# The opening of a fused attention and mixer kernel in another order: identity loaded by itself, first casts on other engines

## The chip, the core and the metric

The kernel runs on one core of a Trainium2 chip. Its time is the device time of one launch, in microseconds (us). The engines of the core are TensorE (PE), VectorE (DVE), ScalarE (ACT), GpSimd (POOL) and SyncE (SP); each works through its own instructions strictly in order and waits on semaphores for the others. SP, ACT and POOL also issue DMA transfers: SP and ACT each have a hardware queue, POOL a queue that is written by software. PE multiplies 16-bit matrices of 128 rows; a matmul takes about one column per clock, and the clock has two levels, 1.2 and 2.4 GHz.

## What is computed

The reference is attention with sliding windows, then a token mixer and a channel mixer, for 8 batches of 576 positions and 8 heads of 64:

```python
scores = scale * np.matmul(q, k.transpose(0, 1, 3, 2))          # per batch and head
mask_plain = (rel >= 0) & (rel < 32)                            # heads 0 to 3
mask_dil = (rel >= 0) & (rel < 128) & (rel % 4 == 0)            # heads 4 to 7
attn = softmax(np.where(masks, scores, -1e9)); attn_out = attn @ v
x = attn_out as (8, 576, 512)
h = np.maximum(xt @ w_tok1, 0.0) @ w_tok2                       # xt: x transposed, 576 -> 256 -> 576
u = x + h.transpose(0, 2, 1)
h2 = np.maximum(u @ w_ch1, 0.0) @ w_ch2                         # 512 -> 1536 -> 512
out = u + h2
```

Inputs and outputs are fp32; inside, operands are fp16 and sums fp32.

## The kernel before

**Staging.** One batch at a time goes through: load of q, k, v; casts to fp16 (`c_q`, `c_k`, `c_t` for the last 64 positions of q and k, `vv` and `vt` for the values); transposes by PE against an identity matrix (`tp_q`, `tp_k`, `tp_t`), copied to `qz` and `kt`; score products for pairs of heads (`sc`, `sm`) with a mask added by a product with `veil`; exponentials on ACT (`attp`, `attd`, `attt`); values times weights (`av`, value steps `va[0]` to `va[7]`, one for each head), divided by the row sum into `xn` on DVE; token mixer (`h1p`, then `h` by relu; `up`, then u); transposes of u (`uT`); and the channel mixer (`gp`, `gt` into hidden, `yp`, `yx`, `yw` out of it). The first matrices of the channel mixer (L941) and the last (L783) are the bulk of PE's work.

**What sets the order.** Nothing is scheduled by a tool: program order on each engine is the order of the source. For batch 0 there is nothing to overlap with, so its attention and token mixer, the *opening*, are written out one by one (L1009 to L1143). From there on `interleave(gen_main(b), steps)` merges the channel mixer of batch b with the attention of batches b+1 and b+2: each step carries a program time, such as `at(8.5, 0.7, dma_steps(b + 2))`, and is put where the running sum of PE's costs reaches it. These numbers only place instructions; at run time semaphores decide.

**The opening before.** POOL first issues the load of `const` (L1009: 672 columns: identity, permutation `perm`, mask band and tails, 168 KB), then clears buffers. SP issues the loads of q and v, ACT those of k. The hardware queues of SP and ACT rotate through 8 semaphores in the order of issue, so that a ninth transfer's issue waits until the transfer eight places earlier has landed; SP's loads of v (L211) stand behind such waits. PE runs nine products of the cleared buffer `idle` (`warm(9)`, L1004), then the transposes of head pair 0 (`tp(0)`), three more of the idle products, the scores of pair 0, and so on. The casts `c_q`, `c_k` of pair p are called by `cast_qk(0, "q", p, engine)`. `warm` does no useful work: it only keeps PE running.

**Names in what follows.** The heads go in pairs 0 to 3. In the list `ts` step 5p is `tp_q` of pair p, 5p+1 `tp_k` (L313), 5p+2 and 5p+3 the two halves of its scores (L427 mask, L429 product), 5p+4 its tails (`sm`). `first_tails` is `tp_t` and the copies of the tails (L415 to L422). `natural_w1` (L1073) reorders the first token matrix by products with `spread`. `emit_h1` is L637 and L639; `u_half(s, half)` makes one block of u (L1115 to L1123). `gate` (L1025) is a one-element copy on POOL into batch 1's load buffer, from `w2p`, so that SP's loads of batch 1 start behind it. `load_w3` are POOL's loads of the channel matrix. Behind the gate come POOL's casts of batch 1, in the order in which PE needs them.

Of the kernel before, what the change touches and what calls it, by code (L numbers as in the profile page):

```python
# [68 lines left out]
def kernel(  # L69
# [936 lines left out]
    ctx.enter_context(tc.manual_schedule())  # L1006


    nc.gpsimd.dma_start(out=const, in_=const_dram)  # L1009
    emit_fixed()  # L1010
    new_qk(0)
    load_qk(0, "q", 0, 2, nc.sync)
    load_qk(0, "k", 0, 2, nc.scalar)
    load_qk(0, "q", 2, 4, nc.sync)
    load_qk(0, "k", 2, 4, nc.scalar)
    load_tail(0, "q", nc.sync)
    load_tail(0, "k", nc.scalar)
    load_qk(0, "q", 4, 8, nc.sync)
    load_qk(0, "k", 4, 8, nc.scalar)
    spark = fixed("spark", [1, 1], FP32)  # L1020
    nc.scalar.activation(out=spark, in_=idle[0:1, 0:1], func=AF.Exp)
    load_v(0)

    def gate(t, src):
        nc.gpsimd.tensor_copy(out=t, in_=src)  # L1025
# [1 line left out]
    def load_w3(i):  # L1027
        c = slice(512 * i, 512 * i + 512)
        nc.gpsimd.dma_start(out=w3[i], in_=moe_w_ch1[:, c].rearrange("(x p) c -> p x c", p=128))

    cast_qk(0, "q", 0, nc.scalar)
    cast_qk(0, "k", 0, nc.vector)
    nc.vector.tensor_scalar(out=veil, in0=const[:, 256:CW], scalar1=1.0, scalar2=60000.0,
                            op0=ALU.subtract, op1=ALU.mult)
    cast_qk(0, "q", 1, nc.gpsimd)
    emit_fixed_late()
    cast_tails_qk(0, nc.gpsimd)
    nc.gpsimd.dma_start(out=w1p, in_=moe_w_tok1[0:512, :].rearrange("(m r) j -> m r j", r=4))
    for hp in range(2, 4):
        cast_qk(0, "q", hp, nc.gpsimd)  # L1040
    nc.gpsimd.dma_start(out=w1t[0][0:64], in_=moe_w_tok1[512:S, :])
    nc.gpsimd.tensor_copy(out=spread[:, 3:515:4], in_=ident)
    cast_qk(0, "k", 3, nc.gpsimd)
    for s in range(4):
        cast_vn(0, s, nc.gpsimd)
    nc.gpsimd.dma_start(out=w2a[:, :, 0:S], in_=moe_w_tok2.rearrange("(p j) t -> p j t", j=2))
    load_w3(0)
    cast_vd(0, 0, nc.gpsimd)
    cast_vd(0, 2, nc.gpsimd)
    load_w3(1)  # L1050
    cast_vx(0, nc.gpsimd)
    nc.gpsimd.dma_start(out=w1t[1][64:128], in_=moe_w_tok1[512:S, :])
    for jb in range(2):
        nc.gpsimd.tensor_copy(
            out=w2p[jb], in_=w2[jb][:, 0:512].rearrange("p (m r) -> p r m", r=4))

    warm(9)
# [3 lines left out]
    def tp(hp):
        ts[5 * hp]()
        ts[5 * hp + 1]()

    def sc(hp):
        for i in range(2, 5):
            ts[5 * hp + i]()

    def natural_w1(i):
        p = bank("main", 3, f"w1_p{i}")  # L1070
# [3 lines left out]
                                 lhsT=spread[:, 128 * s + 3 - r:128 * s + 131 - r], rhs=w1p[:, r],  # L1074
                                 start=(r == 0), stop=(r == 3))
        copy(nc.scalar, w1n[:, 2 * i:2 * i + 2].rearrange("p s j -> p (s j)"), p)

    tp(0)
    warm(3)
    ts[2]()  # L1080
    ts[3]()
    cast_qk(0, "k", 1, nc.vector)
    tp(1)
    first_tails()
    ts[7]()
    ts[8]()
    cast_qk(0, "k", 2, nc.vector)
    ts[10]()
    ts[4]()
    ts[9]()  # L1090
    ts[11]()
    tp(3)
    cast_tail_v(0, nc.vector)
    sc(2)
    natural_w1(0)
    va[0]()
    va[1]()
    sc(3)
    va[2]()
    va[3]()  # L1100
    natural_w1(1)
    for h in range(4, 8):
        va[h]()


    h1 = [sb.tile([128, DM], FP16, tag="h1", bufs=4, name=f"h1_0_{jb}") for jb in range(2)]
# [29 lines left out]
    for s in (1, 2):
        u_half(s, 1)
    for cb in (1, 2, 3):
        emit_uT(0, cb)
# [120 lines left out]
```

## Time and profile before

| what | value |
|---|---|
| runs (us) | 311.51, 277.65, 276.34; median 277.65 |
| profiled execution | 275.95 us, of which the span of its instructions is 274.1 us |
| PE busy in the span | 265.5 us (97%), 2694 matmuls |
| DVE, ACT, POOL busy | 168.4, 148.7, 159.9 us |
| chain that ended last | PE 89%, DMA 5%, DVE 2%, SP's queue 1%, ACT 1% |
| DMA | 54.98 MB, mean 201 GB/s |

The span is the time from the first instruction to the last; 1.85 us of the execution lie around it. An engine's busy time counts only instructions that do work. The chain is followed back from the last instruction, at each step to what released it, so that its shares say which engine's work or which transfer set the time there. Of the profile's 40 slices the first shows PE busy to six tenths, the second and the sixth to eight, the others up to the 39th to nine or more, and the last to four.

### The profile page before, as it was taken

What the parts mean: (1) busy time and instruction counts of PE and PEld (TensorE: products, weight loads), DVE (VectorE), ACT (ScalarE), POOL (GpSimd) and SP (SyncE); (2) the same over time, 40 slices, a digit from 0 to 9 for tenths busy, and PEclk for the clock granted to TensorE, in tenths of its full rate; (3) what the DMA queues carried; (4) which work ended last, traced back from release to release, by engine and by line L of the source; (5) the groups of instructions that cost most, each with busy time, mean ns of one, the idle gap of its engine ahead of it and who ended that gap; (6) DMA issues with size and microseconds to landing.
All of it is one profiled execution on the core that took longest, in us unless ns stands there. A gap on an engine that the chain in (4) does not pass through costs nothing.

```text
span 274.1 us, 6762 instructions
## 1 busy us (share of the span) xinstructions
PE 265.5 (97%) x2694; PEld 197.3 (72%) x2694; DVE 168.4 (61%) x340; ACT 148.7 (54%) x291; POOL 159.9 (58%) x216
## 2 busy tenths in 40 slices
PE   6899989999999999999999999999999999999994
PEld 2787676898676876687776876787776866786673
DVE  6667668676567656595557553875475464961363
ACT  2864675353674655467545666576646565236500
POOL 8871761289868659659974689749970870000000
PEclk9999999999999999999999999999999999999999
DMA  7999999995999799999999899979999040525015
GB/s 220 269 240 231 295 236 207 295 241 150 347 172 219 159 295 198 308 181 240 300 231 214 260 258 255 193 138 330 326 180 152 3 154 2 99 79 149 0 41 153
DMA packets 111471, 54.98 MB, mean 201 GB/s; under 512 B 82736, under 2 KB 107312, under 8 KB 111440
## 3 DMA queue, kind: packets, MB, share of 16 engines
q1 hardware_dynamic: 106784, 49.10, 77.0%
q0 software_dynamic: 2640, 3.94, 8.1%
q10 hardware_dynamic: 2016, 1.51, 1.8%
q8 instruction: 21, 0.34, 0.5%
q14 instruction: 10, 0.08, 0.1%
HBM read 37.59 MB, written 9.44 MB: 172 GB/s over the span
## 4 chain that ended last, share of the span: by engine, by line
PE 89%; DMA 5%; DVE 2%; SPq 1%; ACT 1%; issue 0%; ACTq 0%; POOL 0%
PE gp L941 30%; PE yx L783 13%; PE yw L783 9%; PE h1p L639 5%; PE up L651 4%; PE gt L932 4%; PE yp L969 4%; PE yp L752 4%; PE sc L524 3%; DMA lt<-in_k_dram 3%; DMA l_vx<-in_v_dram 2%; PE h1p L637 1%; PE av L621 1%; SPq L211 1%; PE av L616 1%; PE up L662 1%
## 5 line engine op out<-in xcount | busy, mean ns | idle before, releaser
L109 ACT ACTIVATE gt<-gp 128x512 f16<-128x512 f32 x89 | 53.3, 598 | 49.8 <-PE gp L941 49.5
L783 PEld LDWEIGHTS <-gt 128*128 128x128 f16 x600 | 57.0, 98 | 8.2
L941 PE MATMUL gp<-utd,w 128*128 128x512 f16 x144 | 54.7, 380 | 0.0
L941 PE MATMUL gp<-utm,w 128*128 128x512 f16 x144 | 54.6, 379 | 0.0
L941 PEld LDWEIGHTS <-w 128*128 128x128 f16 x384 | 39.0, 113 | 19.8 <-issue 0.5
L115 POOL TENSOR_TENSOR attp<-attp,const 128x1280 f16<-128x1280 f16 x12 | 31.6, 2637 | 22.1 <-ACT attp L549 22.1
L739 DVE TENSOR_TENSOR gt<-gt 128x768 f16<-128x768 f16 x56 | 32.5, 610 | 12.5 <-ACT gt L109 12.1
L115 DVE TENSOR_TENSOR xn<-av,rec 128x320 f16<-128x320 f32 x64 | 31.5, 492 | 2.2
L115 POOL TENSOR_TENSOR attd<-attd,const 128x1024 f16<-128x1024 f16 x12 | 25.5, 2127 | 5.9 <-issue 5.1
L941 PE MATMUL gp<-uT,w 128*128 128x512 f16 x96 | 25.8, 379 | 0.0
L796 DVE TENSOR_TENSOR o<-yx,u 128x512 f32<-128x512 f32 x22 | 15.2, 691 | 11.6 <-PE yx L783 11.4
L549 ACT ACTIVATE attp<-sc 128x480 f16<-128x480 f32 (+1 forms) x36 | 15.9, 538 | 8.8 <-PE sc L524 8.8
L783 PE MATMUL yx<-w,gt 128*128 128x256 f16 x168 | 20.6, 273 | 0.0
L783 PE MATMUL yx<-wsum_a,gt 128*128 128x256 f16 x168 | 20.6, 273 | 0.0
L657 DVE TENSOR_TENSOR u<-up,xn 128x512 f16<-128x512 f32 x26 | 17.8, 689 | 4.1 <-PE up L651 4.1
L628 DVE RECIPROCAL rec<-av 128x5 f32<-128x5 f32 x64 | 12.3, 192 | 12.7 <-PE av L625 12.6
L105 POOL CAST c_k<-l_k 128x512 f16<-128x512 f32 x29 | 17.6, 615 | 2.2 <-DMA l_k<-in_k_dram 1.1
L666 DVE TENSOR_TENSOR u16t<-up,xn 64x512 f16<-64x512 f32 x7 | 4.8, 690 | 20.8 <-PE up L662 20.8
L105 POOL CAST c_q<-l_q 128x512 f16<-128x512 f32 x26 | 16.3, 633 | 1.9 <-DMA l_q<-in_q_dram 1.2
L870 ACT COPY utd<-utm 128x512 f16<-128x512 f16 x12 | 12.7, 1125 | 8.8 <-DMA u<-utd 4.2
L109 ACT ACTIVATE h<-h1p 128x256 f16<-128x256 f32 x31 | 11.8, 384 | 9.5 <-PE h1p L639 9.1
L806 DVE TENSOR_TENSOR o<-yw,o 128x512 f32<-128x512 f32 x13 | 9.0, 692 | 10.2 <-PE yw L783 10.1
(159 smaller groups left out, 551.3 us busy)
## 6 DMA issues: line engine op xcount, KB each, us to landing
l_q<-in_q_dram SPq DMA_DIRECT2D x15, 512.0 KB, 6.4
l_k<-in_k_dram SPq DMA_DIRECT2D x14, 512.0 KB, 7.1
out_dram<-o SPq DMA_DIRECT2D x12, 512.0 KB, 4.6
l_vn<-in_v_dram SPq DMA_DIRECT2D x32, 128.0 KB, 6.8
l_vd<-in_v_dram SPq DMA_DIRECT2D x16, 256.0 KB, 5.1
w<-in_moe_w_ch_dram POOLq DMA_DIRECT2D x6, 512.0 KB, 7.8
out_dram<-o SPq DMA_DIRECT2D x17, 128.0 KB, 2.6
l_vt<-in_v_dram SPq DMA_DIRECT2D x8, 256.0 KB, 5.5
```

The costliest lines, as they stand in the source:

```text
L105: eng.tensor_copy(out=out, in_=in_)
L109: nc.scalar.activation(out=out, in_=in_, func=AF.Relu)
L115: eng.tensor_tensor(out=out, in0=x, in1=y, op=ALU.mult)
L549: nc.scalar.activation(out=out, in_=in_, func=AF.Exp, scale=0.125)
L628: nc.vector.reciprocal(out=rec[:, :, 0], in_=av[:, :, 64])
L639: nc.tensor.matmul(out=p, lhsT=w[:, s, j], rhs=x[:, s, c], start=False, stop=(s == 3))
L657: nc.vector.tensor_tensor(out=u16(b, s), in0=blocks4(p), in1=blocks4(xn[b][:, s]), op=ALU.add)
L739: nc.vector.tensor_tensor(out=out, in0=x, in1=y, op=op)
L783: nc.tensor.matmul(out=p, lhsT=gta[:, k0 + mb, r:r + 128], rhs=weights[:, mb, c], start=(first and not mb and (not a or len(parts) > 2)), ...
L796: nc.vector.tensor_tensor(out=o[i][:, :, 256 * j:256 * j + 256].rearrange("p s (x c) -> p s x c", x=2), in0=grid(p), in1=u, op=ALU.add)
L870: nc.scalar.copy(out=natural(uTd[:, cb - 2]), in_=uTm[i][:, cb].rearrange("p r m -> p m r"))
L941: nc.tensor.matmul(out=p, lhsT=w3_block(cb, mb), rhs=uT[(b, cb)][0], start=(i == 0), stop=(i == 3))
```

## The change

The opening is written in another order, and the numbers of the later batches are others. The identity (columns 0 to 127 of `const`, 32 KB) is loaded by itself on ACT's queue, the other 544 columns on POOL's. The cast `c_q` of pair 0 goes from ACT to DVE, `c_k` of pair 0 from DVE to POOL. The blocks of u, the steps of the scores and the loads of `w3` stand in other places. For the later batches the diff shows the numbers.

```diff
-    nc.gpsimd.dma_start(out=const, in_=const_dram)
-    emit_fixed()
...
-    cast_qk(0, "q", 0, nc.scalar)
-    cast_qk(0, "k", 0, nc.vector)
...
-    cast_qk(0, "q", 1, nc.gpsimd)
-    emit_fixed_late()
-    cast_tails_qk(0, nc.gpsimd)
...
-    tp(0)
-    warm(3)
-    ts[2]()
-    ts[3]()
-    cast_qk(0, "k", 1, nc.vector)
-    tp(1)
-    first_tails()
...
+    clear_gaps(attp[0])
+    nc.gpsimd.memset(idle, 0.0)
+    load_qk(0, "q", 0, 2, nc.sync)
+    nc.vector.memset(qza[0:64, :, 1], 0.0)
+    nc.gpsimd.dma_start(out=const[:, 128:], in_=const_dram[:, 128:])
...
+    load_qk(0, "k", 2, 4, nc.scalar)
+    load_tail(0, "q", nc.sync)
+    nc.scalar.activation(out=spark, in_=idle[0:1, 0:1], func=AF.Exp)
+    nc.scalar.dma_start(out=const[:, 0:128], in_=const_dram[:, 0:128])
+    nc.gpsimd.memset(vv[0][:, :, :, 64:65], 1.0)
+    load_tail(0, "k", nc.scalar)
+    load_qk(0, "k", 4, 8, nc.scalar)
...
+    cast_qk(0, "k", 0, nc.gpsimd)
+    nc.vector.memset(attt, 1.0)
+    nc.gpsimd.memset(spread, 0.0)
+    clear_gaps(attp[1])
+    cast_tails_qk(0, nc.gpsimd)
+    cast_qk(0, "q", 0, nc.vector)
+    cast_qk(0, "q", 1, nc.gpsimd)
...
+    ts[0]()
...
+    warm(3)
+    ts[1]()
+    cast_qk(0, "k", 1, nc.vector)
+    ts[2]()
+    ts[5]()
+    ts[6]()
+    first_tails()
+    ts[7]()
+    cast_qk(0, "k", 2, nc.vector)
+    ts[8]()
+    ts[9]()
+    ts[10]()
+    ts[3]()
...
-    for s in (0, 2):
-        u_half(s, 0)
...
-    for s in (4, 1, 3):
-        u_half(s, 0)
-    for s in (4, 3, 0):
-        u_half(s, 1)
+    u_half(2, 0)
+    u_half(3, 0)
+    u_half(4, 0)
+    emit_h1(0, 0, 1, h1[0])
+    emit_h1(0, 1, 1, h1[1])
+    u_half(1, 0)
+    u_half(0, 0)
+    u_half(3, 1)
+    u_half(4, 1)
+    u_half(0, 1)
...
-                steps += at(14.6 + late / 6, 0.0, [lambda b=b: u_natural(b)])
+                steps += at(12.75 + late / 6, 1.6, [lambda b=b: u_natural(b)])
...
-                    b + 1, 5.4 + late / 6, 8.2 + late / 6, 10.6 + late / 6, 22.4 + late, 0.9, 4.1, 1.0)
+                    b + 1, 5.0 + late / 6, 8.75 + late / 6, 10.6 + late / 6, 23.2 + late, 0.9, 4.95, 0.4)
...
-                steps += at(2.0, 0.6, cast_steps(b + 2)) + score_steps(b + 2, 21.4 if b % 2 else 18.0, 8.4 if b % 2 else 6.4)
+                steps += at(2.15, 0.95, cast_steps(b + 2)) + score_steps(b + 2, 20.2 if b % 2 else 18.4, 6.1 if b % 2 else 6.4)
...
-                steps += at(8.5, 0.7, dma_steps(b + 2)) + at(12.0, 0.4, places[:4])
-                steps += at(19.6 if b % 2 else 17.2, 0.0, places[4:])
+                steps += at(7.7, 0.8, dma_steps(b + 2)) + at(15.0, 0.0, places[:4])
+                steps += at(19.2 if b % 2 else 17.2, 2.85, places[4:])
...
-                steps += at(17.6, 0.9, load_steps(b + 3))
+                steps += at(19.1, 2.0, load_steps(b + 3))
```

The queue of ACT at the start, before, in the order in which ACT takes it (`lt` holds the last 64 positions of q and k; `spark` is one exponential that makes ACT load its table):

```order
L194 DMA l_k<-in_k_dram 128x2x256 x2
L200 DMA lt<-in_k_dram 64x8x64
L194 DMA l_k<-in_k_dram 128x4x256
L1021 ACT_TABLE_LOAD
L1021 ACTIVATE spark<-idle 1x1
L103 CAST c_q<-l_q 128x512
L103 COPY qz<-tp_q 64x512 x2
```

The same place of ACT's queue with the change:

```order
L194 DMA l_k<-in_k_dram 128x2x256 x2
L1068 ACT_TABLE_LOAD
L1068 ACTIVATE spark<-idle 1x1
L1069 DMA const<-consts 128x128
L200 DMA lt<-in_k_dram 64x8x64
L194 DMA l_k<-in_k_dram 128x4x256
L103 COPY qz<-tp_q 64x512 x2
```

The load of the table, `spark` and the new load of the identity now stand ahead of the load of `lt`, and the cast of `c_q` is gone from this engine.

On POOL, from the first cast of the opening to the loads behind it, before (the cast `c_q` at the top is pair 1's; `c_t` is the cast of `lt`):

```order
L105 CAST c_q<-l_q 128x512
L177 MEMSET vv 128x40
L178 MEMSET vt 64x4
L179 MEMSET w1t 128x256
L177 MEMSET vv 128x40
L178 MEMSET vt 64x4
L179 MEMSET w1t 128x256
L180 MEMSET w 128x2x64
L105 CAST c_t<-lt 128x512
L1038 DMA w1p<-in_moe_w_tok_dram 128x1024
L105 CAST c_q<-l_q 128x512 x2
```

The same part of POOL's program with the change:

```order
L105 CAST c_k<-l_k 128x512
L1086 MEMSET spread 128x515
L1021 MEMSET attp 128x8x128
L105 CAST c_t<-lt 128x512
L105 CAST c_q<-l_q 128x512
L1091 MEMSET vv 128x40
L1093 MEMSET w 128x2x64
L1095 MEMSET w1t 128x256
L1096 MEMSET vt 64x4
L1097 DMA w1p<-in_moe_w_tok_dram 128x1024
L105 CAST c_q<-l_q 128x512
```

The cast `c_q` of pair 1 has gone behind `c_t`, which reads both tails; `c_k` of pair 0 has come to the top; four of the small memsets now stand between `c_q` of pair 1 and the load of `w1p`.

## Rows read from the trace of the kernel before

**Rows 1.** Stretches: from:to, length, then busy us (instructions) of each engine, clock, DMA.

```profile
10.00:12.00 2.00, 1.50 (x23) 1.29 (x22) 1.73 (x6) 1.91 (x5) 1.73 (x4) 1.00 1.31 249
...
28.00:45.00 17.00, 16.24 (x199) 11.67 (x198) 11.38 (x26) 11.37 (x23) 10.13 (x20) 1.00 1.12 250
45.00:260.00 215.00, 215.00 (x2136) 159.79 (x2133) 130.58 (x258) 121.95 (x236) 131.56 (x155) 1.00 0.87 198
260.00:274.10 14.10, 10.43 (x96) 8.18 (x93) 7.23 (x15) 0.00 (x0) 0.00 (x0) 1.00 0.32 94
```

**Rows 2.** Chain that ended last, its longest piece: start, length, what.

```profile
1.80 7.03 DMA lt<-in_k_dram
```

**Rows 3.** Timeline of PE: start, length, line, operation, count, [idle before <-releaser].

```profile
2.54 4.02 PE L1004 MATMUL idle_p<-idle 128*128 128x512 f16 x9 [2.54 <-POOL idle L164]
6.60 0.59 PE L313 MATMUL tp_q<-const,c_q 128*128 128x128 f16 x4
...
7.40 1.05 PE L1004 MATMUL idle_p<-idle 128*128 128x512 f16 x3
...
8.40 0.24 PE L429 MATMUL sc<-qz,kt 128*128 128x160 f16 x1
...
9.17 0.39 PE L313 MATMUL tp_q<-const,c_q 128*128 128x128 f16 x4
...
10.56 0.24 PE L429 MATMUL sc<-qz,kt 128*128 128x160 f16 x1 [0.49 <-DVE kt L318]
...
13.58 0.25 PE L429 MATMUL sc<-qz,kt 128*128 128x128 f16 x1 [0.26 <-DVE kt L318]
...
19.49 0.19 PE L625 MATMUL av<-vt,attt 128*128 128x65 f16 x1 [0.53 <-POOL vt L105]
...
31.57 0.39 PE L313 MATMUL tp_k<-const,c_k 128*128 128x128 f16 x4
```

**Rows 4.** DMA transfers by issue: what, queue, count, KB, us from issue to landing.

```profile
l_k<-in_k_dram ACTq DMA_DIRECT2D x1, 256.0 KB, 4.7
const<-consts POOLq DMA_DIRECT2D x1, 168.0 KB, 5.3
...
lt<-in_k_dram ACTq DMA_DIRECT2D x1, 128.0 KB, 7.0
...
w1t<-in_moe_w_tok_dram POOLq DMA_DIRECT2D x1, 32.0 KB, 5.2
```

**Rows 5.** Timeline of ACT and DVE in the first 16 us, columns as in PE's.

```profile
0.73 1.03 ACTq L194 DMA_DIRECT2D l_k<-in_k_dram  x2
...
3.44 1.28 ACT L1021 ACT_TABLE_LOAD   x1 [3.44 <-issue]
...
5.97 0.35 DVE L105 CAST c_k<-l_k 128x512 f16<-128x512 f32 x1
...
7.65 0.69 DVE L318 COPY kt<-tp_k 128x512 f16<-128x512 f16 x1 [0.74 <-PE tp_k L313]
...
15.41 0.45 DVE L105 CAST vv<-l_vt 128x512 f16<-128x512 f32 x1 [1.29 <-DMA l_vt<-in_v_dram]
```

**Rows 6.** Timeline of POOL, the same columns.

```profile
8.88 0.61 POOL L105 CAST c_t<-lt 128x512 f16<-128x512 f32 x1 [0.80 <-DMA lt<-in_k_dram]
...
14.13 0.72 POOL L1046 DMA_DIRECT2D w<-in_moe_w_tok_dram  x1
...
21.30 0.18 POOL L1025 CAST lt<-w2p 1x1 f32<-1x1 f16 x1
...
30.09 1.17 POOL L105 CAST c_k<-l_k 128x512 f16<-128x512 f32 x2 [0.17 <-DVE gt L111]
```

**Rows 7.** Timeline of PE and ACT in an odd batch.

```profile
146.70 2.75 PE L752 MATMUL yp<-w,gt 128*128 128x512 f16 x12
...
147.39 1.08 ACT L103 COPY kt<-kr 128x512 f16<-128x512 f16 x1
...
149.38 0.65 PE L524 MATMUL sc<-qt,kt 64*128 64x160 f16 x14
```

More of the change, by code (lines that the diff above doesn't have):

```diff
@@ L1006 @@
     ctx.enter_context(tc.manual_schedule())
-    nc.gpsimd.dma_start(out=const, in_=const_dram)
-    emit_fixed()
     new_qk(0)
[L1012 to L1019, printed above, removed]
     spark = fixed("spark", [1, 1], FP32)
-    nc.scalar.activation(out=spark, in_=idle[0:1, 0:1], func=AF.Exp)
-    load_v(0)
+    v_loads = load_v_steps(0)
     def gate(t, src):
@@ L1029, in load_w3, with clear_gaps, make_veil @@
         nc.gpsimd.dma_start(out=w3[i], in_=moe_w_ch1[:, c].rearrange("(x p) c -> p x c", p=128))
-    cast_qk(0, "q", 0, nc.scalar)
-    cast_qk(0, "k", 0, nc.vector)
-    nc.vector.tensor_scalar(out=veil, in0=const[:, 256:CW], scalar1=1.0, scalar2=60000.0,
-                            op0=ALU.subtract, op1=ALU.mult)
-    cast_qk(0, "q", 1, nc.gpsimd)
-    emit_fixed_late()
-    cast_tails_qk(0, nc.gpsimd)
[L1038 to L1057, printed above, removed]
+    def clear_gaps(a):
+        nc.gpsimd.memset(a.rearrange("p h (b c) -> p h b c", c=PST)[:, :, :, 128:PST], 0.0)
+    def make_veil():
+        nc.vector.tensor_scalar(out=veil, in0=const[:, 256:CW], scalar1=1.0, scalar2=60000.0,
+                                op0=ALU.subtract, op1=ALU.mult)
     ts = [st[2] for st in score_steps(0, 0.0, 1.0)]
     va = [st[2] for st in value_steps(0, 0.0, 1.0)]
[L1061 to L1067, printed above, removed]
+    h1 = [sb.tile([128, DM], FP16, tag="h1", bufs=4, name=f"h1_0_{jb}") for jb in range(2)]
     def natural_w1(i):
@@ L1076, in natural_w1 @@
         copy(nc.scalar, w1n[:, 2 * i:2 * i + 2].rearrange("p s j -> p (s j)"), p)
-    tp(0)
-    warm(3)
-    ts[2]()
-    ts[3]()
-    cast_qk(0, "k", 1, nc.vector)
-    tp(1)
-    first_tails()
[L1085 to L1106, printed above, removed]
     def u_half(s, half):
@@ L1123, in u_half @@
             nc.vector.tensor_tensor(out=t[rows], in0=blocks4(p[rows]), in1=blocks4(xn[0][rows, s, c]), op=ALU.add)
-    for jb in range(2):
-        emit_h1(0, jb, 0, h1[jb])
-    for s in (0, 2):
-        u_half(s, 0)
-    for jb in range(2):
-        emit_h1(0, jb, 1, h1[jb])
-    for s in (4, 1, 3):
-        u_half(s, 0)
-    for s in (4, 3, 0):
-        u_half(s, 1)
-    emit_uT(0, 0)
[L1136 to L1139, printed above, removed]
+    clear_gaps(attp[0])
@@ new lines @@
+    nc.gpsimd.memset(idle, 0.0)
+    load_qk(0, "q", 0, 2, nc.sync)
+    nc.vector.memset(qza[0:64, :, 1], 0.0)
+    nc.gpsimd.dma_start(out=const[:, 128:], in_=const_dram[:, 128:])
+    nc.vector.memset(qza[64:128, :, 0], 0.0)
+    load_qk(0, "k", 0, 2, nc.scalar)
+    load_qk(0, "q", 2, 4, nc.sync)
+    nc.gpsimd.memset(vt[1][64:128], 0.0)
+    load_qk(0, "k", 2, 4, nc.scalar)
+    load_tail(0, "q", nc.sync)
+    nc.scalar.activation(out=spark, in_=idle[0:1, 0:1], func=AF.Exp)
+    nc.scalar.dma_start(out=const[:, 0:128], in_=const_dram[:, 0:128])
@@ new lines @@
+    nc.gpsimd.memset(vv[0][:, :, :, 64:65], 1.0)
+    load_tail(0, "k", nc.scalar)
+    load_qk(0, "k", 4, 8, nc.scalar)
+    load_qk(0, "q", 4, 8, nc.sync)
+    v_loads[0]()
+    nc.gpsimd.memset(vt[0][64:128], 0.0)
+    v_loads[1]()
+    v_loads[2]()
+    v_loads[3]()
+    v_loads[4]()
+    v_loads[6]()
+    v_loads[5]()
+    nc.gpsimd.memset(vt[0][0:64, :, 64:65], 1.0)
+    nc.gpsimd.memset(w1t[0], 0.0)
+    cast_qk(0, "k", 0, nc.gpsimd)
+    nc.vector.memset(attt, 1.0)
+    nc.gpsimd.memset(spread, 0.0)
@@ new lines @@
+    clear_gaps(attp[1])
+    cast_tails_qk(0, nc.gpsimd)
+    cast_qk(0, "q", 0, nc.vector)
+    cast_qk(0, "q", 1, nc.gpsimd)
+    nc.gpsimd.memset(vv[1][:, :, :, 64:65], 1.0)
+    v_loads[7]()
+    nc.gpsimd.memset(w2a[:, :, S:640], 0.0)
+    make_veil()
+    nc.gpsimd.memset(w1t[1], 0.0)
+    nc.gpsimd.memset(vt[1][0:64, :, 64:65], 1.0)
+    nc.gpsimd.dma_start(out=w1p, in_=moe_w_tok1[0:512, :].rearrange("(m r) j -> m r j", r=4))
+    cast_qk(0, "q", 2, nc.gpsimd)
+    nc.gpsimd.tensor_copy(out=spread[:, 3:515:4], in_=ident)
@@ new lines @@
+    cast_qk(0, "q", 3, nc.gpsimd)
+    cast_qk(0, "k", 3, nc.gpsimd)
+    cast_vn(0, 0, nc.gpsimd)
+    nc.gpsimd.dma_start(out=w1t[0][0:64], in_=moe_w_tok1[512:S, :])
+    cast_vn(0, 2, nc.gpsimd)
+    cast_vn(0, 3, nc.gpsimd)
+    cast_vn(0, 1, nc.gpsimd)
+    nc.gpsimd.dma_start(out=w2a[:, :, 0:S], in_=moe_w_tok2.rearrange("(p j) t -> p j t", j=2))
+    load_w3(0)
+    cast_vd(0, 0, nc.gpsimd)
+    cast_vd(0, 2, nc.gpsimd)
+    warm(9)
+    cast_vx(0, nc.gpsimd)
+    load_w3(1)
+    nc.gpsimd.tensor_copy(out=w2p[1], in_=w2[1][:, 0:512].rearrange("p (m r) -> p r m", r=4))
@@ new lines @@
+    ts[0]()
+    nc.gpsimd.tensor_copy(out=w2p[0], in_=w2[0][:, 0:512].rearrange("p (m r) -> p r m", r=4))
+    nc.gpsimd.dma_start(out=w1t[1][64:128], in_=moe_w_tok1[512:S, :])
+    warm(3)
[11 more added lines that the diff above has]
+    ts[3]()
+    ts[11]()
+    ts[15]()
+    ts[16]()
+    ts[4]()
+    cast_tail_v(0, nc.vector)
+    ts[12]()
+    ts[13]()
@@ new lines @@
+    ts[14]()
+    natural_w1(0)
+    va[0]()
+    va[1]()
+    ts[17]()
+    ts[18]()
+    ts[19]()
+    va[2]()
+    va[3]()
+    natural_w1(1)
+    va[4]()
+    va[5]()
+    va[6]()
+    va[7]()
+    emit_h1(0, 0, 0, h1[0])
+    emit_h1(0, 1, 0, h1[1])
+    u_half(2, 0)
[8 more added lines that the diff above has]
+    u_half(0, 1)
+    emit_uT(0, 0)
+    u_half(1, 1)
+    u_half(2, 1)
@@ L1142 @@
+    emit_uT(0, 1)
+    emit_uT(0, 3)
+    emit_uT(0, 2)
     new_qk(1)
```

## The prediction

> **What bounds the kernel now.** I read the stretches first. From 45 to 260 us PE is busy 215.00 of 215.00 us at the full clock [rows 1]: a reader should see that nothing there can be won by another order of the same matmuls, and the change keeps them all. The end, 14.1 us with PE busy 10.43, has no step that moves. What is left is the opening and its handover to batch 1 (28 to 45: PE 16.24 of 17.00). The chain of waits names what sets the opening: the transfer of k's tails, from its issue at 1.80 to its landing at 8.83 [rows 2]. PE's timeline then gives the size of each wait: it idles 0.49 us ahead of the product at 10.56, 0.26 ahead of 13.58 and 0.53 ahead of 19.49 [rows 3]. So the question is where the start of the channel mixer, near 27 us, goes; behind it every microsecond counts once.
>
> The sum is made against the profiled execution, 275.95 us (span 274.1, and 1.85 around it). The median of the runs shown is 277.65, the faster of the other two 276.34. Two per cent, about what a measurement of this kernel can tell from no change, is 5.5 us.
>
> **Identity.** Before, it landed with all of `const`, at 1.22 + 5.3 = 6.5, and PE's first transposes began at 6.60 [rows 3, 4]. Now ACT issues two loads of k (until 1.76), loads its table (1.28) and then issues the identity's 32 KB, at about 3.2 [rows 5]. Below, it can't come ahead of the load of k in front of it on that queue, which was issued near 1.25 and took 4.7: 5.95 [rows 4, 5]. Above, the nearest transfer of the same size took 5.2, which gives 8.4 [rows 4]. I go by the queue itself: the tails' 128 KB, in the same rows of 256 bytes, landed 2.88 behind that load of k; a quarter of the bytes, a quarter of the time, 0.7: 6.7. The cast of `c_q` on DVE is hidden: it takes the slot of `c_k` there, 5.97 to 6.32 [rows 5]. First transposes at 6.75: **+0.15**.
>
> The Trainium skill, "DMA: Bandwidth & Descriptors", section "Anatomy of one DMA — SWDGE (gpsimd) path", gives a fit of about 2.0 us plus bytes over 436 GB/s. By it the identity would land near 5.3 and the transposes begin with the cast, at 6.4, 0.2 earlier than before. The trace doesn't bear it out in this stretch: 32 KB took 5.2 and 168 KB 5.3 on POOL's own queue.
>
> **First scores.** `warm(3)`, 1.05 us, now stands between `tp_q` and `tp_k` of pair 0. Before, it lay behind both and hid the copy to `kt` [rows 3]; now nothing hides that copy. The two transposes took 0.80 together (6.60 to 7.40), so `tp_k` moves from 7.0 to 6.75 + 0.4 + 1.0 = 8.15. The copy began 0.65 behind it [rows 5]; at the full clock four transposes take 0.39 and not 0.59 [rows 3], so say 0.45 now: 8.6 to 9.3, first product at 9.3 and not 8.40, **+0.9**. `c_k` of pair 0 goes to POOL, 0.61 like `c_t` [rows 6]; its data are there by 4.5 and it is needed at 8.15, so it costs nothing unless POOL's memsets run three microseconds late. The mask's columns now go second on POOL; even 1 us late they land near 7.6, ahead of 9.3.
>
> **Pair 1.** On POOL `c_q` of pair 1 now stands behind `c_t`, which needs k's tails. On ACT these now stand behind the table and the identity. Below: 8.0; `const` now starts about 1 us later on POOL, and its 168 KB at the profile's mean of 201 GB/s are 0.84 us of the transfers that shared the time with the early loads. Above: issued near 3.7, 7.0 on the way as before [rows 4], 10.7. I take the identity's 0.7 on top of 8.83: 9.55, since the queue was busy from the first load on. Two casts of 0.61 [rows 6] and `tp_q` of pair 1 starts at 10.85, not 9.17: **+1.65**. PE has only half of pair 0's scores to do until then (0.4, from 9.3 to 9.7): a **new wait of about 1.1 us**. Transposes, copy and product follow as before, 10.56 + 1.65 = 12.2 [rows 3].
>
> **Pair 2.** Until 13.58 before there were 3.02 us, 0.26 of them idle [rows 3]. The second half of pair 0's scores, 0.4, is new in there, and `tp_q` of pair 2 stands behind pair 1's tails, so that DVE gets its copies later. Between 0 (all of it under DVE's copies) and 0.4 (none) I take 0.35: pair 2 **+2.0**.
>
> **Given back.** The values of the dilated heads waited 0.53 for `vt`, whose data came late; when PE comes 2 us later, they are there. The cast of `l_vt`, done at 15.86 [rows 5], released the first values; what PE lost there lies between 0 and the 0.26 of its neighbour; I take 0.2. The new order of u's blocks puts another block behind the relu; from -0.3 to +0.3, I take -0.2. The start of the channel mixer: 2.0 - 0.53 - 0.2 - 0.2 = **+1.05**.
>
> **Handover to batch 1.** POOL's load of the second token matrix goes from 14.13 to about 16.0: tails 0.7, the cast of pair 1 that is now behind them 0.6, four small memsets that were ahead of them about 0.6. `w2p` and the gate at 21.30 [rows 6] follow, to about 23.2, or 23.7 with the load that now stands right ahead of the gate. SP's loads of batch 1 are all queued behind the gate. Their first cast of `c_k` was done at 30.7 (30.09 + 0.61), its transposes began at 31.57 [rows 3, 6]: 0.87 to spare, 1.9 with PE's own delay. A shift of 1.9 to 2.4 costs 0 to 0.5: **+0.2**.
>
> **Later batches.** An odd batch's first group of dilated scores stands four matmuls earlier, 2.75 / 12 × 4 = 0.9. ACT's copy to `kt` ended at 148.47, the scores began at 149.38 [rows 7]: just enough. If it isn't, a wait of at most the copy's 1.08 in each of two batches. Loads that stand later behind SP's output stores have most of a batch to spare. I take 0 (bounds 0 and +2.2; a gain is excluded by PE's 215.00).
>
> **Sum:** 1.05 + 0.2 = +1.25, so 275.95 + 1.25 = **277.2**.
>
> **Rivals.**
>
> *The opening gets shorter.* If the early loads gain what `const` took from them, the tails land near their lower end, 8.0. Pair 1 starts at 9.7, held by its first scores and the two casts, not by 1.1 us of waiting; pair 2 comes at most 0.5 later, and the waits that vanish (0.53 + 0.2) and u's 0.2 make it -0.4 to -0.9. Time 275.3. For it: PE's order now has work for each copy of DVE. Against it: the tails were the last to land before, and two more things stand ahead of them. Chance 0.24.
>
> *The other side: batch 1's loads.* If identity and tails come at their upper ends (8.4 and 10.7), POOL's program shifts by 1.2 more, the gate goes to about 24.7, 3.4 later than before; pair 1's start goes to 12.0, and the mixer to +2.2. The transposes of batch 1's k then lack 3.4 - 0.87 - 2.2 = 0.3, and each later cast of POOL, which follow each other closely, keeps the lag. 2.2 + 0.3 to 1.3 gives 278.5 to 279.5. It decides at 0.87 us: a gate that is later than PE's mixer by more than that stops PE. For it: the 5.2 us of 32 KB. Against it: the transfers of one queue share its time, so a late issue costs less than it is late. Chance 0.16.
>
> *The clock falls back.* The products at the start ran at the lower level, 4.02 us for nine [rows 3]. PE now idles about 0.9 and 1.1 us between 8.5 and 10.85 with 0.4 of work between. From 10 to 12, PE was busy 1.50 of 2.00 us and the clock stayed at 1.00 [rows 1], which speaks against it; but that stretch was denser. At the lower level five microseconds of matmuls cost 2.5 more; less what waits hide, 279.3. Chance 0.06. The Trainium skill, "TensorE: Matmul & The Clock Gate", section "Why this matters for your kernels", warns that idle gaps between bursts of matmuls take PE back to its slow clock, which speaks against an order with two such waits; before, no row shows such a fall.
>
> *It doesn't do what it says:* the identity lands no earlier than the whole `const` did, because it is queued behind k. That is already my forecast.
>
> **How the numbers follow.** The forecast of 277.2 has 0.50 (its own range 276.2 to 278.5), the rivals 0.24, 0.16 and 0.06, other mishaps of the later batches 0.04. The range runs from the shorter opening's lower part, 274.9, to the late loads' upper end, 279.5. No case reaches 5.5 us but several together: faster 0.02, same 0.94, slower 0.04.
>
> **What would show it.** Right: first transposes at 6.6 to 6.9 and `tp_k` behind the three idle products; PE's wait ahead of `tp_q` of pair 1, released by POOL's `c_q`; no wait for `vt` near 20; the gate near 23; PE full from 45 to 260. Wrong: tails that land before 8.9 (then the first rival), `tp_k` of batch 1 waiting for POOL by over half a microsecond (the second), a clock under 1.00 near 11 (the third), or idle PE in the dilated scores of the odd batches.

## The result and the profile after

The changed kernel took 280.44 us (median of 6 runs, 279.79 to 281.71) beside 277.24 of the kernel before: a ratio of 1.0131, interval 1.0094 to 1.0168, or 3.6 us more. It is slower, as forecast, and within 2%, but above the range that was given (up to 279.5) and three times the forecast step (+1.25). Ratios leave disturbed runs out: for one experiment below too few were left for a ratio, and the profiles of 5, 6, 8 and 10 are of such runs (287 to 288 us), so that the lengths of those four profiles aren't compared with the others'.

The stretches of the changed kernel's profile (span 278.6), columns as in [rows 1]:

```profile
10.00:12.00 2.00, 1.23 (x12) 0.78 (x11) 1.13 (x2) 0.33 (x1) 1.66 (x5) 1.00 1.23 283
28.00:45.00 17.00, 15.63 (x180) 10.84 (x178) 10.60 (x22) 11.21 (x23) 10.50 (x20) 1.00 1.11 255
45.00:260.00 215.00, 213.19 (x2132) 158.35 (x2130) 134.97 (x261) 120.53 (x233) 134.71 (x156) 1.00 0.86 201
260.00:279.00 19.00, 14.89 (x135) 11.43 (x132) 8.92 (x18) 2.64 (x5) 0.00 (x0) 0.97 0.23 70
```

Two things changed: PE does less from 28 to 45 us (15.63 for 16.24), and it has lost 1.81 us in the middle, which was full before. The chain that ended last says where, among its longest pieces:

```profile
2.57 7.64 DMA lt<-in_k_dram
25.10 8.24 DMA l_k<-in_k_dram
...
125.28 2.82 DVE gt L739
```

k's tails are on it as before, 7.64 us and from a later issue; a load of batch 1 is new on it, and one sum of DVE. PE's timeline, against [rows 3]:

```profile
2.20 4.02 PE L1004 MATMUL idle_p<-idle 128*128 128x512 f16 x9 [2.20 <-POOL idle L1058]
7.77 0.59 PE L313 MATMUL tp_q<-const,c_q 128*128 128x128 f16 x4 [1.54 <-DMA const<-consts]
8.15 1.48 PE L1004 MATMUL idle_p<-idle 128*128 128x512 f16 x3
9.43 0.63 PE L313 MATMUL tp_k<-const,c_k 128*128 128x128 f16 x4
10.85 0.31 PE L429 MATMUL sc<-qz,kt 128*128 128x160 f16 x1 [0.65 <-DVE kt L318]
11.76 0.40 PE L313 MATMUL tp_q<-const,c_q 128*128 128x128 f16 x4
13.16 0.24 PE L429 MATMUL sc<-qz,kt 128*128 128x160 f16 x1 [0.49 <-DVE kt L318]
16.64 0.24 PE L429 MATMUL sc<-qz,kt 128*128 128x128 f16 x1 [0.26 <-DVE kt L318]
...
21.71 0.19 PE L625 MATMUL av<-vt,attt 128*128 128x65 f16 x1
...
34.16 0.40 PE L313 MATMUL tp_k<-const,c_k 128*128 128x128 f16 x4 [0.19 <-POOL c_k L105]
```

Read it downward: PE is 1.17 us late at the first transposes (6.60 before), 2.45 at the first score product, 2.6 at pair 1, 3.06 at pair 2; the wait for `vt` is gone; at batch 1's first transposes of k it is 2.59 late (31.57 before). A second sign is in the lengths: the three idle products took 1.48 and not 1.05, four transposes 0.59 and 0.63, a score product 0.31; only from 11.76 on are they 0.40 and 0.24. PE stood at 1.2 GHz until then; before, four transposes took 0.39 from 9.17 on. The clock column shows 1.00 in this early stretch all the same, so the level is read from the lengths here.

The identity's 32 KB, next to the other columns and k's tails (columns as in [rows 4]):

```profile
const<-consts POOLq DMA_DIRECT2D x1, 136.0 KB, 5.5
lt<-in_k_dram ACTq DMA_DIRECT2D x1, 128.0 KB, 7.6
const<-consts ACTq DMA_DIRECT2D x1, 32.0 KB, 5.5
```

And ACT's queue at the start, then POOL's casts of the tails and of pair 1, the gate, and batch 1's first cast:

```profile
1.79 1.28 ACT L1068 ACT_TABLE_LOAD   x1 [1.79 <-issue]
2.19 0.35 ACTq L1069 DMA_DIRECT2D const<-consts  x1
2.57 0.69 ACTq L200 DMA_DIRECT2D lt<-in_k_dram  x1
```

```profile
10.34 0.61 POOL L105 CAST c_t<-lt 128x512 f16<-128x512 f32 x1 [2.09 <-DMA lt<-in_k_dram]
10.89 0.81 POOL L105 CAST c_q<-l_q 128x512 f16<-128x512 f32 x1
...
22.86 0.18 POOL L1014 CAST lt<-w2p 1x1 f32<-1x1 f16 x1
30.69 0.61 POOL L105 CAST c_t<-lt 128x512 f16<-128x512 f32 x1 [7.65 <-DMA lt<-in_k_dram]
```

The identity was issued at 2.19, earlier than I had thought (the queue doesn't wait for the table's load to end), and landed at 7.7. The tails, issued at 2.57 and not at 1.80, landed at 10.2 and not at 8.83; POOL's whole program moved behind them, the gate by 1.56. POOL's cast of pair 1's `c_q` ended at 11.70, and the transposes of pair 1 began at 11.76: of all that comes late at the start, the tails set the way on from here, though PE's own work ended just ahead of them, at 11.64.

### The profile page after: what moved, and what is told of

It reads as the page before. It is cut to its first block, busy times and chain, and to the rows that moved or that the text cites. A ratio compares the mean times of both kernels' runs of the same rounds, so it can differ in the third digit from the quotient of the medians.

```text
span 278.6 us, 6751 instructions
## 1 busy us (share of the span) xinstructions
PE 266.2 (96%) x2694; PEld 197.3 (71%) x2694; DVE 173.5 (62%) x340; ACT 148.4 (53%) x290; POOL 164.7 (59%) x217
## 4 chain that ended last, share of the span: by engine, by line
PE 82%; DVE 8%; DMA 6%; issue 1%; POOL 1%; ACT 1%; ACTq 0%; POOLq 0%; DVEq 0%
PE gp L941 27%; PE yx L783 12%; PE yw L783 8%; PE up L651 4%; PE h1p L639 4%; PE gt L932 4%; PE yp L752 4%; PE yp L969 4%; DMA l_k<-in_k_dram 3%; DMA lt<-in_k_dram 3%; PE sc L524 3%; DVE gt L739 2%; PE av L616 1%; PE av L621 1%; PE h1p L637 1%
## 5 line engine op out<-in xcount | busy, mean ns | idle before, releaser
L739 DVE TENSOR_TENSOR gt<-gt 128x768 f16<-128x768 f16 x56 | 36.9, 689 | 12.6 <-ACT gt L109 12.3
L105 POOL CAST c_k<-l_k 128x512 f16<-128x512 f32 x30 | 20.1, 678 | 2.3 <-DMA l_k<-in_k_dram 2.3
L105 POOL CAST c_t<-lt 128x512 f16<-128x512 f32 x8 | 4.9, 612 | 17.8 <-DMA lt<-in_k_dram 17.8
```

What stands on the lines that cost most here:

```text
L105: eng.tensor_copy(out=out, in_=in_)
L739: nc.vector.tensor_tensor(out=out, in0=x, in1=y, op=op)
```

## The experiments

They were run beside the kernel before, 1 to 8 on one chip and 9 to 12 on another; the changed kernel itself was measured apart from them, so that they are compared with it by the ratios to before. "Marker" is the start of batch 1's first transposes of k, in one profile of each: 31.57 before and 34.16 with the change in the profiles above; 32.34 and 32.46 where the opening was the old one (the second and the twelfth experiment).

| run | marker | ratio to before (interval) |
|---|---|---|
| 1 new opening, old later times | 36.35 | 1.0117 (1.0070 to 1.0163) |
| 2 old opening, new later times | 32.34 | 0.9997 (0.9963 to 1.0030) |
| 3 identity first | 33.98 | 1.0115 (1.0060 to 1.0170) |
| 4 `c_q` of pair 1 ahead | 34.68 | 1.0065 (1.0035 to 1.0095) |
| 5 both of these | 35.01 | 1.0059 (1.0030 to 1.0089) |
| 6 second `w3` behind the gate | 35.47 | 1.0111 (1.0070 to 1.0153) |
| 7 all three | 33.44 | 1.0037 (1.0004 to 1.0070) |
| 8 thirteen idle products | 34.93 | 1.0087 (1.0058 to 1.0117) |
| 9 waits filled | 33.90 | 1.0064 (1.0031 to 1.0098) |
| 10 constants whole | 33.81 | none |
| 11 best order found | 33.16 | 1.0054 (1.0024 to 1.0084) |
| 12 before, second `w3` late | 32.46 | 1.0004 (0.9980 to 1.0028) |

### 1 and 2: the two halves of the change

```diff
# 1: the changed kernel, in the loop over the later batches
-                steps += at(19.1, 2.0, load_steps(b + 3))
+                steps += at(17.6, 0.9, load_steps(b + 3))
...
# and so all lines of the change's last part; 2: the kernel before, the same lines the other way
```

> The changed opening with the program times of the later batches as before. Theory A (opening and later batches each lose by themselves): the mixer of batch 0 starts near 29.8 as in the changed kernel, 2.7 later than before, and no multiply of DVE on line 739 takes longer than 1.5 us, PE is full from 45 to 260; span near 277.0, +2.6 to +3.0 on before, ratio 1.010. Rival B (the wait of 1.8 us at 126.96 comes from the later loads, which the opening shifts): the wait is there too, span near 278.6.

> The opening as before with the changed program times of the later batches. Theory A: the mixer of batch 0 starts at 27.1, and near 124 us a sum of DVE on line 739 starts about 0.1 us behind a POOL mask multiply of 2.6 us, takes 2.9 us, and PE waits 1.8 us for an output sum; span near 275.9 to 276.1, ratio 1.007. Rival B: no such wait, span 274.1, ratio 1.000. Rival C (the program times cost or gain in many small places): no single wait over 1 us, but a loss or gain spread over the batches.

The opening alone costs 1.17%, 3.3 us on 277.8, as much as the whole change within the intervals; the new times alone cost nothing that can be told (-1.0 to +0.8 us). Theory A was half right: the long wait near 127 us wasn't there in 1, but it didn't come with the new times in 2 either (its longest wait behind the opening was 0.95). So, as far as one profile of each can tell, that wait belongs to one execution's timing and not to the numbers. In 1 PE's late start was worse than forecast, and the lengths say why:

```profile
8.09 0.58 PE L313 MATMUL tp_q<-const,c_q 128*128 128x128 f16 x4 [1.86 <-DMA const<-consts]
...
12.15 0.61 PE L313 MATMUL tp_q<-const,c_q 128*128 128x128 f16 x4
...
16.07 0.61 PE L313 MATMUL tp_q<-const,c_q 128*128 128x128 f16 x4
...
17.61 0.39 PE L313 MATMUL tp_q<-const,c_q 128*128 128x128 f16 x4
```

Behind the wait of 1.86 us for the identity, four transposes take 0.6 until past 16 us and 0.49 at 17.28: PE ran at the lower level until then. The changed kernel has the same opening, and in its profile the level was up by 11.76; so the level differs between executions of one opening. It is what most of the lateness of 1 comes from: pair 1 starts 0.39 us later than in the changed kernel's profile (12.15 for 11.76), the mixer 1.91 later (31.70 for 29.79). The 1.5 us between them are an estimate of what the longer stretch at the lower level costs.

### 3, 4 and 5: the two waits of the opening

```diff
# 3
+    nc.scalar.dma_start(out=const[:, 0:128], in_=const_dram[:, 0:128])
     load_qk(0, "k", 0, 2, nc.scalar)
...
-    nc.scalar.dma_start(out=const[:, 0:128], in_=const_dram[:, 0:128])
# 4
+    cast_qk(0, "q", 1, nc.gpsimd)
     cast_tails_qk(0, nc.gpsimd)
     cast_qk(0, "q", 0, nc.vector)
-    cast_qk(0, "q", 1, nc.gpsimd)
# 5: both
```

> The changed kernel with the identity's load first on ACT's queue, ahead of the loads of k. Both theories: it lands before 6, the first transposes start near 6.45 instead of 7.77, and the idle products behind them are over by 8.2. Theory A (pair 1 is held by k's tails as well): tails land near 10.2, the cast of q of pair 1 ends near 11.7, its transposes start at 11.6 to 11.8 as in the changed kernel, PE idles about 2 us ahead of them; mixer of batch 0 at 29.4 to 29.8, ratio to the changed kernel 0.999 to 1.000. Rival D (the identity alone makes the opening late): everything behind moves by 1.3 to 2.2, mixer at 27.6 to 28.5.

> The changed kernel with POOL's cast of q of pair 1 ahead of the cast of the tails, which waits for k's tails. Theory A (two chains end together near 11.7): the cast ends by 9, pair 1's transposes start right behind the first scores, at 11.5 to 11.7, so at most 0.25 is won; mixer at 29.5 to 29.8. Rival E (the order of the two casts alone makes the opening late): mixer 1 us or more earlier, at 28.8 or before.

> The changed kernel with the identity first on ACT's queue and the cast of q of pair 1 ahead of the cast of the tails. Theory F (a second chain ends at the same time: k's tails, POOL's program behind their cast, its loads, the gate, the loads and casts of batch 1): the mixer of batch 0 starts at 27.4 to 28.3, 1.5 to 2.4 earlier than in the changed kernel, but POOL's first cast of q of batch 1 still ends at 32 to 32.7, PE waits 1.2 to 2.2 us ahead of batch 1's first transposes, and the time is within 0.7 us of the changed kernel's. Rival D (PE's own opening is the whole loss): PE doesn't wait there for over 0.5 us and the time falls by 1.5 to 2.4, to 1.005 of before.

In 3 the identity's DMA took 2.5 us; PE's timeline:

```profile
6.48 0.40 PE L313 MATMUL tp_q<-const,c_q 128*128 128x128 f16 x4 [0.26 <-DVE c_q L105]
...
10.84 0.40 PE L313 MATMUL tp_q<-const,c_q 128*128 128x128 f16 x4 [1.31 <-POOL c_q L105]
...
32.47 0.40 PE L313 MATMUL tp_q<-const,c_q 128*128 128x128 f16 x4 [0.86 <-POOL c_q L105]
```

The first transposes gain 1.3 us, and the wait moves on: to pair 1, which waits 1.31 for POOL's cast behind the tails, and to batch 1, where PE waits 0.86 for POOL. The total is unchanged. Three of my numbers were off: the tails came at 9.5 and not 10.2, pair 1 at 10.84, and the mixer at 28.9, between the forecasts of the two theories. In 4 the profile did what theory A said of pair 1 (11.50, marker no earlier; the mixer at 30.0, a little later than forecast), but the time fell to 1.0065, more than its 0.25 us; 5 does no better than 4, and PE waits 1.36 us at batch 1's first transposes, as theory F said, though its mixer starts at 29.4 and not by 28.3, and its time falls by 2 us, as rival D said. Two late chains end together at batch 1, but they don't explain the sizes. What 4 and 5 both take away is the cast of `c_q` behind the tails, and with it a wait of PE at pair 1. That this wait is what they gain is argued and not shown: the changed kernel's own profile hardly has it (PE's work ends at 11.64 there, pair 1 begins at 11.76), the profile of 6, with the same opening, has 1.14 us of it.

### 8 and 9: the clock

```diff
# 8
-    warm(9)
+    warm(13)
# 9
-    warm(9)
+    warm(15)
...
     ts[2]()
+    warm(2)
+    warm(2)
+    warm(1)
     ts[5]()
```

> The changed kernel with thirteen idle products at the start instead of nine, which fill PE until the identity lands near 7.7. Theory A (the idle 1.5 us keeps PE at the 1.2 GHz level longer): the level rises by 8.3, the three idle products behind the first transposes take 0.7 to 1.0 instead of 1.48, the first score product starts at 9.9 to 10.3 instead of 10.85; pair 1 still starts at 11.4 to 11.8 behind POOL's casts, so the time stays within 0.4 us of the changed kernel's. Rival G (the low level itself is the loss): mixer of batch 0 at 29.0 or earlier. If the level is set by time alone, the three products still take 1.48.

> The changed kernel with fifteen idle products at the start instead of nine and five more between the first scores of pair 0 and the transposes of pair 1: PE has something to do in both of the waits that the changed order makes, and no transfer or cast comes earlier. Theory H (PE's clock stays at or goes back to 1.2 GHz because of these waits): from the first transposes on four transposes take 0.39 everywhere and no 0.6, and the time falls by 0.8 to 2 us from the changed kernel's, to a ratio of 1.006 to 1.010. Rival A (the transfers alone set the start of each pair): ratio unchanged at 1.012 to 1.015.

In 8 the level rose early as theory A said (four transposes of pair 0 in 0.38, three idle products in 0.81), but behind the 1.34 us that PE then waited at pair 1 it fell again: the transposes of pair 1 took 0.61. By the ratios its time is 1.2 us below the changed kernel's and not within 0.4, which the intervals don't tell apart. In 9, where both waits are filled with products that compute nothing, no four transposes take over 0.40, no transfer or cast is earlier (identity at 8.0, tails at 10.4), and the ratio goes from 1.0131 to 1.0064: 1.9 us by the middles. With the intervals of both, 0.5 to 3.2 us; both forecasts of theory H hold. The mean granted clock of the runs behind the ratios fits: none of 9's is below 0.997, as before, while two of the changed kernel's six stand at 0.987. But the clock alone doesn't put the kernels in order, since runs of 4 go down to 0.985 at a ratio of 1.0065. And the two profiles don't show the gain: from pair 1 on, 9 runs as the changed kernel does (pair 1 at 11.75 and 11.76, marker at 33.90 and 34.16), because POOL's `c_q` ends at 11.69 and 11.70. So what 9 gains must lie in executions whose level stays low or falls, as in the profiles of 1 and 6; how many of the changed kernel's are of that kind isn't known. PE's transposes of pair 1 in 9, and its stretch:

```profile
11.75 0.40 PE L313 MATMUL tp_q<-const,c_q 128*128 128x128 f16 x4
```

```profile
10.00:12.00 2.00, 1.85 (x15) 1.01 (x16) 0.40 (x2) 0.57 (x1) 1.47 (x5) 1.00 1.20 281
```

### 6 and 7: the loads of batch 1

```diff
# 6
-    load_w3(1)
...
     gate(l32[(1, "t")][0:1, 0, 0:1], w2p[1][0:1, 0, 0:1])
+    load_w3(1)
# 7: 5 and 6 together
```

> The changed kernel with POOL's second load of the channel matrix (512 KB) behind the gate, so that it no longer stands ahead of batch 1's loads. Theory F: batch 1's tails land 1 to 2 us earlier than 30.55, its first cast of q ends near 31, and since PE's opening is as late as before, at most 0.6 us is won. If the loads of batch 1 set all, 1.5 to 2 are won. If the 512 KB come too late themselves, PE waits for them in the fifth block of the mixer, near 33.

> The edits of the two kernels before together: identity first, cast of q of pair 1 ahead of the tails, second load of the channel matrix behind the gate. Theory F: both chains are shorter, mixer at 27.4 to 28.3, first cast of q of batch 1 done by 31, so the time falls by 1.5 to 2.5 us from the changed kernel, to a ratio of 1.002 to 1.006 to before, though neither edit alone gives over 0.7. Rival: the gains simply add, or neither shows, because a third wait (casts of k of pair 2 and 3 of batch 1) takes their place.

6 won nothing: batch 1's tails were cast at 31.99 (30.69 with the change), no earlier. Its stretches show the clock column itself at work, since here the level had risen before it fell; PE's waits of the same time stand in front of them:

```profile
7.71 0.38 PE L313 MATMUL tp_q<-const,c_q 128*128 128x128 f16 x4 [1.48 <-DMA const<-consts]
...
9.75 0.24 PE L429 MATMUL sc<-qz,kt 128*128 128x160 f16 x1 [0.72 <-DVE kt L318]
...
11.59 0.61 PE L313 MATMUL tp_q<-const,c_q 128*128 128x128 f16 x4 [1.14 <-POOL c_q L105]
```

```profile
8.00:10.00 2.00, 1.28 (x14) 0.74 (x12) 1.36 (x3) 1.16 (x2) 0.24 (x1) 0.99 1.13 279
10.00:12.00 2.00, 0.86 (x9) 0.55 (x8) 0.03 (x1) 0.57 (x1) 1.63 (x5) 0.50 1.22 284
12.00:16.00 4.00, 3.77 (x35) 3.48 (x34) 2.19 (x5) 2.56 (x5) 4.00 (x11) 0.50 1.27 230
16.00:18.00 2.00, 2.00 (x30) 1.91 (x28) 1.67 (x4) 1.32 (x4) 2.00 (x5) 0.81 0.85 214
```

PE idled 1.48 us for the identity, worked a little, idled 0.72 for the copy to `kt`, and from 10 to 16 us the granted clock was 0.50; the 1.14 us for pair 1 came when it had already fallen. Three of the four runs behind 6's ratio have a mean clock of 0.986 to 0.988; 7 us at 0.50 in 279 make 0.987, so that such a stretch was in them too, by this estimate. 7, without a wait of over 0.5 us in the opening, kept the upper level from 7 us on (three idle products in 0.81, all later transposes 0.39 or 0.40) and is the best of the changed orders, 1.0037: 1.0 us over before, and 1.0 us is also how much later its marker is (33.44 against 32.4). Theory F's ratio and start of the mixer (28.3) hold. Its other end doesn't: batch 1's first cast of q was done at 31.9 and not by 31, and PE still waits 0.85 us for it; nor does it hold for 5 that one edit alone gives under 0.7.

### 10, 11 and 12: whole constants, and a better kernel

```diff
# 10: the changed kernel
+    nc.gpsimd.dma_start(out=const, in_=const_dram)
     nc.gpsimd.memset(idle, 0.0)
+    clear_gaps(attp[0])
...
-    nc.scalar.dma_start(out=const[:, 0:128], in_=const_dram[:, 0:128])
# 11: 7, and
+    ts[1]()
     warm(3)
-    ts[1]()
# 12: the kernel before
-    load_w3(1)
...
     gate(l32[(1, "t")][0:1, 0, 0:1], w2p[1][0:1, 0, 0:1])
+    load_w3(1)
```

> The changed kernel with the constants loaded whole, 168 KB first on POOL, as before; all else as changed. Theory: they land near 6.5, first transposes at 6.6 and no wait of 1.5 us there; k's tails land near 8.9, pair 1 starts at 10.1 to 10.4, held by the cast of q behind the cast of the tails; mixer 1 to 1.6 us earlier than in the changed kernel, ratio to before 1.004 to 1.008. Rival (the load by itself isn't the cause, the queue is late anyway): first transposes at 7.5 or later, ratio 1.011 or more.

> The edits of the third combined kernel (identity first, cast of q of pair 1 ahead of the tails, second load of the channel matrix behind the gate), and the three idle products behind both transposes of pair 0 again instead of between them. Theory: first score product at 8.4 to 8.6 instead of 9.0, pair 1 still bound by the cast of the tails and DVE, so at most 0.5 us better than the combined kernel: ratio to before 0.999 to 1.004. Rival: the mask's columns (second on POOL) come last, product at 9.0 as there, no gain.

> The kernel before with POOL's second load of the channel matrix behind the gate. Theory F: batch 1's tails land about 1 us earlier, and since PE has 0.87 us to spare there already, nothing is won where PE's own opening is last: ratio 0.997 to 1.000. Rival: the fifth block of the mixer waits for the matrix, ratio 1.003 or more.

10 has no ratio; its profile shows first transposes at 6.48, as expected, but the tails at 9.9 and not 8.9: they were issued at 2.52, behind the load of the table, and not at 1.80. Pair 1 waited 1.64 us and ran at the lower level (0.60 for four transposes). So the wait at pair 1 needs no identity: it comes from the tails' later issue and from `c_q` standing behind them. 11 was no better than 7; its rival was right, the mask's columns came last (PE waited 0.40 for `veil`, first product at 9.58), and 1.0054 is above its forecast. 12 is the same as before, as expected, though batch 1's tails were cast later (28.79 for 27.32) and not 1 us earlier. None of the kernels beats the one before.

## Why the prediction was wrong

**The base.** The sum was added to one execution of the kernel before, 275.95, in which PE had no wait from 45 to 260 us. The median of its runs is 277.24. Of the 3.2 us between the forecast of 277.2 and the measured 280.44, 1.3 are this base; the other 1.95 are a step that was larger than +1.25. Put on 277.24, the stated range would have reached to 280.8.

**Identity: the step that failed first.** The price lay between 5.95 and 8.4 and I took 6.7, by "a quarter of the bytes, a quarter of the time" behind the load of k. It landed at 7.7, after 5.5 us, which is the nearest row of that size (32 KB in 5.2 on a busy machine) and not the share of bytes. +0.15 became +1.17. By the fit in the Trainium skill, "DMA: Bandwidth & Descriptors", section "Anatomy of one DMA — SWDGE (gpsimd) path", which is one for POOL's queue and not for ACT's, an estimate would be 2.1 us. The nearest to that is the third experiment, where it stood first and took 2.5. Behind others in the queue it was over twice that.

**Pair 1: the step that failed on the way to the mixer.** The cast of `c_q` behind the tails is late, as forecast, but by 2.59 us and not 1.65. The tails landed at 10.2 and not 9.55: against the prediction's argument that a late issue costs less than it is late, they were issued 0.77 later and landed 1.4 later. The cast behind them took 0.81 and not 0.61. By the ends of POOL's cast (11.70) and of PE's own work (11.64) it is this term, and not the identity, that set pair 1 in the changed kernel's profile; both were late at once. So the new wait of 1.1 us didn't show there; it shows, with 1.31, 1.14, 1.34 and 1.64, in 3, 6, 8 and 10, where PE was earlier.

**The clock: the rival that I thought unlikely.** I gave 0.06 to "the clock falls back", at 279.3, because a stretch with PE busy 1.50 of 2.00 us had kept the upper level [rows 1]. The changed opening has two stretches that are emptier (PE busy 0.46 of 2.00 us from 6 to 8, 1.23 from 10 to 12), and in the profiles of the change and of experiments 1, 4, 6, 8, 10 and 11 PE ran at 1.2 GHz for some microseconds of the opening beyond the start. By the ratios 9 gives back about half of the loss (1.9 of 3.6 us). That the rival's price, 2.1 us over the forecast, is near to it is partly luck: the one profile in which the longer stretch can be priced, that of 1, gives 1.5. The Trainium skill, "TensorE: Matmul & The Clock Gate", section "Why this matters for your kernels", says that idle gaps between bursts bring the slow clock; now the trace agrees (0.50 in the sixth experiment, behind waits of 1.48 and 0.72 us).

**First scores.** `tp_k` moved by 2.45 us, not 1.15: the three idle products in front of it cost 1.28 and ran at the lower level, and the identity's lateness adds 1.17. That nothing hides the copy to `kt` was right (PE waits 0.65). POOL's cast of `c_k` took 2.45 us and not 0.61, but was done at 6.88, still in time.

**Pair 2 and what is given back.** +3.06 for +2.0, from the lateness in front of it; the step itself was 0.46, near the 0.35 taken. The wait for `vt` is gone, as forecast.

**Handover.** The gate went to 22.86 (forecast 23.2). POOL's casts of `c_k` of batch 1 began 3.4 us later (33.49 for 30.09 [rows 6]), which the 0.87 us to spare and PE's own lateness hid nearly whole (a wait of 0.19). That this chain stood ready to take over, the second rival, is what 3 and 5 show (0.86 and 1.36).

**Later batches.** No cost, as forecast, by the ratio of 2; in the changed kernel's own profile there was one wait of 1.80 us that I hadn't thought of (below). PE's waits from 45 to 260 us differ from one profile to the next: none before, 0.4 in 12, which has the same opening, 1.3 in 2, 0.6 in 1, 2.7 in 3. The 215.00 of 215.00, by which the prediction excluded a gain there, belonged to one execution.

The sum at the opening and the handover was +1.25; experiment 1 makes it 3.3. The signs and the places were right; the sizes of the identity's and the tails' terms were not, and the clock stood in the sum with nothing. How the 3.3 us divide among them stays open: 3, which takes away the wait for the identity alone, gains nothing; 4, which takes `c_q` from behind the tails, and 9, which fills the waits and makes no transfer earlier, gain 1.8 and 1.9 by the ratios; the three edits of 7 gain 2.6.

## What to carry to other kernels

Early in a kernel, price a small load by the nearest row of its size in a queue as full, and not by its bytes: 32 KB took 5.5 us behind other loads and 2.5 us ahead of them. Ask which of several late transfers sets the way on: here moving the identity ahead brought the first transposes 1.3 us forward and the total nothing. Count the gaps that a new order leaves on PE before the clock is up or where work is thin, and price them twice, as waits and as work at half speed; if a gap can't be closed, fill it with products, which gave back 1.9 us here by the ratios. Where several chains end close together (transposes, POOL's program, next batch's loads), taking one away shows only the next. Add a forecast step to the middle of several runs and not to the one execution that was profiled.

## What the runs showed of the hardware that was not expected

DVE's sums on line 739 read two fp16 tensors from SBUF; they take about 0.6 us (the middle one 0.56). In the changed kernel's profile one began 0.12 us behind a mask multiply of POOL. POOL, DVE and PE there:

```profile
125.08 2.60 POOL L115 TENSOR_TENSOR attp<-attp,const 128x1280 f16<-128x1280 f16 x1 [0.82 <-ACT attp L549]
```

```profile
125.20 2.90 DVE L739 TENSOR_TENSOR gt<-gt 128x768 f16<-128x768 f16 x1
128.02 0.68 DVE L796 TENSOR_TENSOR o<-yw,u 128x512 f32<-128x512 f32 x1
```

```profile
128.76 1.47 PE L783 MATMUL yw<-wsum_b,gt 128*128 128x256 f16 x12 [1.80 <-DVE o L796]
```

The sum ends 0.4 us behind POOL's multiply, and PE waits for the output sum that stands behind it. In the profile of 11 the same stands at 185.61: a sum that began 0.11 us behind such a multiply took 2.91 us, and PE waited 1.81. Sums that read PSUM (line 796) keep their time beside POOL: in the kernel before, two that began at 94.43 and 95.75 took 0.69 while POOL's multiplies ran from 91.55 to 97.35. In the profile of experiment 5 a sum began about 0.3 us ahead of three POOL multiplies in a row, while a cast of POOL was still running, and lasted until 0.4 us behind the third (the row holds two sums). PE's next products waited 6.82 us for the output sum behind it and then ran at the lower level, twelve in 2.71 us and not in the 1.47 of the row above:

```profile
94.33 7.07 DVE L739 TENSOR_TENSOR gt<-gt 128x768 f16<-128x768 f16 x2
```

```profile
95.20 2.59 POOL L115 TENSOR_TENSOR attp<-attp,const 128x1280 f16<-128x1280 f16 x1
97.75 0.66 POOL L115 TENSOR_TENSOR attt<-attt,const 128x256 f16<-128x256 f16 x1
98.38 2.59 POOL L115 TENSOR_TENSOR attp<-attp,const 128x1280 f16<-128x1280 f16 x1
```

```profile
102.04 2.71 PE L783 MATMUL yw<-w,gt 128*128 128x256 f16 x12 [6.82 <-DVE o L757]
```

The profiles of 6, 8 and 10 have a wait of the same kind (6.86, 5.35 and 6.86 us).

The Trainium skill, "GPSIMD Engine Reference", section "Key points", says that POOL shares its SBUF interfaces with DVE and contends with instructions of two SBUF inputs; the trace agrees, and shows that such an instruction can be held over three of POOL's in a row (in 8 one sum alone took 6.47 us). Here two that met began within 0.3 us of each other. No run took this cost away by itself; that it is the sharing is read from these rows and not shown by an experiment.
